# Routing in two halves: six expert slots that run while the other tokens are routed

## The chip, the cores and the metric

The kernel runs on one core of one Trainium2 chip. The metric is device time in microseconds (us). A kernel's figure is the median of its runs. A kernel's profile is one execution; its span is about 1.7 us shorter than the time of that same run.

PE is TensorE's matmul side, PEld its weight loads, DVE is VectorE, ACT ScalarE, POOL GpSimd, SP SyncE, which issues most loads here. PSUM is the memory in which the matmuls leave their results.

## The reference, cut to what matters

```python
# attention: batch 8, heads 8, sequence 576, head width 64; causal, window 64
attn = softmax(mask(scale * q @ k.T)) @ v            # -> x: (8, 576, 512)
# mixture of experts: 8 experts, hidden width 1024
logits = x @ w_gate
local  = sigmoid(x @ w_local)
for b in range(B):
    prev_e = -1
    for s in range(S):
        fresh_e = argmax(logits[b, s])
        e = fresh_e if s == 0 or local[b, s] < 0.5 else prev_e   # goes on along the sequence
        prev_e = e
        p = softmax(logits[b, s])
        out[b, s] = p[e] * (relu(x[b, s] @ w1[e]) @ w2[e])
```

A token's expert can depend on the token before it, so routing is a scan along each sequence. It isn't a scan across batches: the first four batches can be routed before the other four have left attention. That is what makes the change possible.

## The kernel before

There are 4608 tokens: 36 columns of 128. Attention works through nine chunks of 512 tokens, each in four units (pairs of heads). The loop runs `LEAD` units of scores ahead of the values that use them:

```python
def load(sc):                                   # three kinds of buffer, then va
    vtt = vts[sc] = qp.tile([P, HP, SC], F32, name="vtt")             # 2 of these
    kt = kts[sc] = kp.tile([P, HP, SC], F32, name="kt", bufs=4)
    qt = qts[sc] = qp.tile([P, HP, SC], F32, name="qt", bufs=3)
    ...
load(0)
load(1)
...
for i, (sc, hp) in enumerate(units):
    if hp == 0:
        ...
        if sc + 2 < NSC:
            load(sc + 2)
    if i + LEAD < len(units):
        ps[units[i + LEAD]] = scores(*units[i + LEAD])
    ...
    values(sc, hp, ps.pop((sc, hp)), x, g)      # ends with three operations on DVE
    if hp == 0 and sc + 1 < NSC:
        gated = gates(sc + 1)                   # logits of the next chunk, from vtt
    if hp == HP - 1:                            # a chunk is done: its logits, its rows of x
        nc.vector.tensor_reduce(lt[:, 4 * sc:4 * sc + 4, :], ...)
        nc.gpsimd.dma_start(out=xs[...], in_=x...)
```

Then all tokens are routed at once, by some 90 small operations on DVE and a few matmuls. The last step of it is a table: for each place in the experts' list, which token stands there and with what weight. It is a sum of products of one-hot matrices, so it runs on PE, with rows that DVE builds:

```python
for c in range(C):                              # 36 columns of tokens
    rowh = ...                                  # [128, 128]: row of the place, one-hot
    colh = ...                                  # [128, 2, NS]: slot of the place, times token and weight
    nc.tensor.matmul(tab, lhsT=rowh, rhs=colh, start=(c == 0), stop=(c == C - 1))
```

Last come the experts. A slot is 128 tokens of one expert. Blocks of two slots come first, then blocks of one. Each block gathers its rows of x, fetches the expert's two weight matrices (2 MB each; four buffers for either, used in turn), and does two layers:

```python
st = fetch(0)
turn(st)                                        # transposes the gathered rows
for n in range(sure):
    nxt = fetch(n + 1) if n + 1 < sure else None
    hidden(st)                                  # first layer
    if nxt:
        turn(nxt)
    result(st)                                  # second layer, scaled, scattered to out
    st = nxt
rest = [fetch(n) for n in range(sure, NBLK)]    # blocks that may not be needed
with tc.If(used > SURE):
    ...
```

PE's instructions stand in the order of the program (its schedule is set by hand).

## Time and profile before

| what, in the kernel before | us |
|---|---|
| median time of three runs (span of the profiled one, which took 797.36) | 799.2 (795.6) |
| last matmul of attention ends | 139.3 |
| first expert matmul starts | 216.2 |
| last expert matmul ends | 787.4 |
| granted TensorE clock, mean of the span | 0.946 |

Read it as a sum of four terms: attention, a hole, the experts and an end. In the last 571 us PE has no gap, so whatever the change adds to PE's stream there is added to the time; what it takes out of the hole is gained. The lines that show this stand in the prediction.

The transfers that the page lists include the experts' weights (count, size, median us from issue to landing):

```profile
w<-in_w_dram SPq DMA_DIRECT2D x64, 2048.0 KB, 8.4
```

And the very end: the last of these transfers is issued by SP at 773.4 us, 14 us before the last expert matmul ends, and the last result is scattered by POOL at 788.5; the program ends 7 us after that.

```profile
773.43 0.33 SPq L678 DMA_DIRECT2D w<-in_w_dram  x1
```

```profile
788.47 0.98 POOL L714 DMA_INDIRECT out_dram<-y,idx  x1 [13.03 <-ACTq L731]
```

### The profile page before, as it was taken

The numbers are of one execution on the slowest core, as the hardware profiler recorded it, in microseconds if no ns is written. First come the engines' busy times: TensorE is split into PE (matmuls) and PEld (weight loads), VectorE is DVE, ScalarE is ACT, GpSimd is POOL, SyncE is SP. The second block draws the span as 40 slices with busy tenths as digits, with TensorE's granted clock in tenths as the row PEclk, the third lists the DMA queues.
The fourth block names the chain that finished last, engine by engine and source line by source line (L and its number), as shares of the span: only waits on it lengthen the run. The fifth ranks groups of instructions, "written<-read, shape, count | busy, mean of one in ns | idle before, by whom it ended". The sixth has DMA issues, their size and how long they took to land. (4 is left out here: it accounts for less than half of the span.)

```text
span 795.6 us, 12193 instructions
## 1 busy us (share of the span) xinstructions
PE 710.3 (89%) x5295; PEld 509.8 (64%) x5295; DVE 194.3 (24%) x450; ACT 95.3 (12%) x127; POOL 153.3 (19%) x137
## 2 busy tenths in 40 slices
PE   4887888264499999999999999999999999999995
PEld 3666667054277567657756756766877867768673
DVE  5777778794110011001001001000010010100100
ACT  2233333000000000000100000000100001001000
POOL 4565364102201011111121021111111111111000
PEclk9899999555599999999999999999999999999998
DMA  9999993104995544536455364468888888889883
GB/s 334 387 398 395 398 383 121 53 1 176 424 420 221 211 172 161 222 146 221 162 175 222 133 236 174 156 228 330 321 321 312 332 326 312 326 329 325 311 292 120
DMA packets 37570, 204.61 MB, mean 257 GB/s; under 512 B 3485, under 2 KB 3501, under 8 KB 29312
## 3 DMA queue, kind: packets, MB, share of 16 engines
q1 hardware_dynamic: 28320, 173.45, 59.0%
q0 software_dynamic: 9184, 30.24, 9.5%
q8 instruction: 46, 0.75, 0.4%
q14 instruction: 20, 0.16, 0.1%
HBM read 184.80 MB, written 19.92 MB: 257 GB/s over the span
## 5 line engine op out<-in xcount | busy, mean ns | idle before, releaser
L698 PE MATMUL hp<-xt,w 128*128 128x128 f32 (+1 forms) x1856 | 286.3, 315 | 0.0
L698 PEld LDWEIGHTS hp<-xt,w 128*128 128x128 f32 x1856 | 266.0, 192 | 31.3 <-issue 13.4
L710 PE MATMUL yp<-w,h 128*128 128x512 f32 x640 | 279.5, 592 | 0.0
L710 PEld LDWEIGHTS yp<-w,h 128*128 128x128 f32 x640 | 119.5, 190 | 139.3 <-issue 137.0
L702 DVE TENSOR_SCALAR h<-hp 128x512 f32<-128x512 f32 x40 | 27.6, 691 | 521.7 <-issue 401.3
L714 POOL DMA_INDIRECT out_dram<-y,idx x40 | 40.1, 1003 | 305.2 <-ACT y L713 277.8
L672 POOL DMA_INDIRECT xg<-xs,idx x43 | 42.1, 980 | 257.3 <-PE tp L686 202.7
L713 ACT ACTIVATE y<-yp,pw 128x512 f32<-128x512 f32 x40 | 27.5, 687 | 367.6 <-PE yp L710 357.8
L243 PE MATMUL xo<-vb,p 128*64 128x74 f32 x576 | 47.2, 233 | 12.1 <-issue 6.1
L233 DVE TENSOR_TENSOR p<-p,mask 128x1024 f32<-128x1024 f32 x36 | 52.6, 1466 | 15.4 <-ACT p L230 15.4
L214 PE MATMUL sp<-qt,kt 64*64 64x128 f32 (+1 forms) x1296 | 45.6, 278 | 7.8 <-issue 7.8
L704 ACT ACTIVATE h<-hp 128x512 f32<-128x512 f32 x40 | 23.9, 597 | 224.1 <-PE hp L698 224.1
L243 PEld LDWEIGHTS xo<-vb,p 128*64 128x64 f32 x576 | 40.6, 138 | 15.3 <-issue 8.3
L214 PEld LDWEIGHTS sp<-qt,kt 64*64 64x64 f32 x1296 | 39.3, 143 | 17.3 <-issue 15.3
L243 PE MATMUL xo<-va,p 128*64 128x74 f32 x576 | 47.3, 233 | 2.7 <-issue 2.7
L686 PE MATMUL tp<-ident,xg 128*128 128x128 f32 x160 | 25.6, 296 | 21.7 <-DMA xg<-xs,idx 21.7
L230 ACT ACTIVATE p<-sp 128x1024 f32<-128x1024 f32 x36 | 36.9, 1025 | 61.6 <-PE sp L214 50.7
L243 PEld LDWEIGHTS xo<-va,p 128*64 128x64 f32 x576 | 40.6, 138 | 4.1 <-issue 4.1
L686 PEld LDWEIGHTS tp<-ident,xg 128*128 128x128 f32 x160 | 20.3, 153 | 24.7 <-issue 20.8
L201 POOL COPY vb<-va 64x2368 f32<-64x2368 f32 x9 | 27.0, 2999 | 45.9 <-DVE va L198 45.9
L645 PE MATMUL tab<-colh,rowh 128*128 128x86 f32 x72 | 22.4, 467 | 10.7 <-DVE colh L644 10.7
L687 DVE COPY xt<-tp 128x512 f32<-128x512 f32 x40 | 26.5, 681 | 19.1 <-PE tp L686 19.1
(144 smaller groups left out, 210.1 us busy)
## 6 DMA issues: line engine op xcount, KB each, us to landing
w<-in_w_dram SPq DMA_DIRECT2D x64, 2048.0 KB, 8.4
va<-in_v_dram SPq DMA_DIRECT2D x9, 1184.0 KB, 16.9
vtt<-in_vt_dram SPq DMA_DIRECT2D x9, 1024.0 KB, 16.2
xs<-x POOLq DMA_DIRECT2D x9, 1024.0 KB, 9.8
kt<-in_k_dram SPq DMA_DIRECT2D x8, 1024.0 KB, 16.8
qt<-in_q_dram SPq DMA_DIRECT2D x8, 1024.0 KB, 17.0
kt<-in_k_dram SPq DMA_DIRECT2D x4, 256.0 KB, 6.0
qt<-in_q_dram SPq DMA_DIRECT2D x4, 256.0 KB, 5.8
```

Of the source, the lines that this page charges most:

```text
L201: nc.gpsimd.tensor_copy(vb[:WIN], va[:WIN])
L214: nc.tensor.matmul(sp[c * WIN:(c + 1) * WIN, j, a:b], lhsT=kt[h, hp, block * WIN:(block + 1) * WIN], rhs=qt[h, hp, a:b], start=True, stop= ...
L230: nc.scalar.activation(p, sp, Act.Exp, scale=DH ** -0.5)
L233: nc.vector.tensor_tensor(p, p, m.to_broadcast([P, 2, SC]), op=Alu.mult)
L243: nc.tensor.matmul(xo[par * WIN:(par + 1) * WIN, j, s * VW:(s + 1) * VW], lhsT=p[:, j, b * WIN:(b + 1) * WIN], rhs=w[:, s, 2 * hp + j, :], ...
L672: nc.gpsimd.indirect_dma_start(out=x, out_offset=None, in_=xs[:, :], in_offset=bass.IndirectOffsetOnAxis(ap=idx[:, s:s + 1], axis=0))
L686: nc.tensor.transpose(tp[:, kk, :], x[:, kk * P:(kk + 1) * P], ident)
L698: nc.tensor.matmul(hp[:, i, :], lhsT=st["w1"][:, kk, m * P:(m + 1) * P], rhs=st["xt"][:, kk, :n], start=(kk == 0), stop=(kk == DK - 1))
L702: nc.vector.tensor_relu(o, hp)
L710: nc.tensor.matmul(yp, lhsT=st["h"][:, m, i * P:(i + 1) * P], rhs=st["w2"][:, m, :], start=(m == 0), stop=(m == FK - 1))
L713: nc.scalar.activation(y, yp, Act.Copy, scale=pw[:, s:s + 1])
L714: nc.gpsimd.indirect_dma_start(out=out[:, :], out_offset=bass.IndirectOffsetOnAxis(ap=idx[:, s:s + 1], axis=0), in_=y, in_offset=None, bou ...
```

## The change

The intent is to fill the hole. After the fifth of the nine chunks the first four batches are complete. The change makes routing a Python generator with stops (`yield`) in it. The first half's routing advances by one piece after each unit of attention; from the columns it has routed, six full slots are formed (fewer than the batches surely fill). Their rows and weights are fetched while attention still runs, and they are the first six jobs of the experts. The second half is routed between the pieces of those six jobs. For that the experts' weights and attention's q and k share one ring of four buffers, with two spare ones added when attention is over, so six in place of eight; the turned v gets one buffer in place of two, and one buffer of probabilities goes.

The diff, cut to its core:

```diff
+    with ExitStack() as fast:
+        ring = fast.enter_context(tc.tile_pool(name="ring", bufs=4))
+        rt = Router(fast, tc, lt, tabs, ident)
+        ex = Experts(fast, tc, ring, *moe)
+        attention(tc, ring, q, k, v3, vt, xs, lt, ok, wg2s, ident, rt, ex)
+        ex.run(fast, rt)
     bad = const.tile([1, 1], I32, name="bad")
     flag(tc, ok, bad, ident)
-    route(tc, lt, idx, pw, ej, ident)
-    experts(tc, xs, w1, w2, out, idx, pw, ej, ident)
 ...
     def load(sc):
-        vtt = vts[sc] = qp.tile([P, HP, SC], F32, name="vtt")
-        kt = kts[sc] = kp.tile([P, HP, SC], F32, name="kt", bufs=4)
-        qt = qts[sc] = qp.tile([P, HP, SC], F32, name="qt", bufs=3)
+        both = ring.tile([P, 2, HP, SC], F32, name="w")
+        kt, qt = kts[sc], qts[sc] = both[:, 0], both[:, 1]
 ...
+    def turned(sc):
+        vtt = vts[sc] = kp.tile([P, HP, SC], F32, name="vtt", bufs=1)
+        nc.sync.dma_start(out=vtt, in_=vt[:, :, sc * SC:(sc + 1) * SC])
+
+    turned(0)
     load(0)
     load(1)
     gated = gates(0)
+    turned(1)
 ...
         values(sc, hp, ps.pop((sc, hp)), x, g)
         if hp == 0 and sc + 1 < NSC:
             gated = gates(sc + 1)
+            if sc + 2 < NSC:
+                turned(sc + 2)
+        if side:
+            next(side, None)                     # one piece of the first routing
 ...
+            if side is None and 4 * (sc + 1) >= C1:
+                side = rt.first(psum)
+    for _ in side:
+        pass
+    ex.begin()                                   # fetches of the first two jobs
```

The table is built nine columns in one operation. There is one stop between its rows and its matmuls:

```diff
+        for a in range(0, n, 2 * m):             # m = 9; n = 18 in the first, 36 in the second
+            built = []
+            for b in range(a, min(a + 2 * m, n), m):
+                rowh = ...                       # [128, 9, 128] on DVE
+                colh = ...                       # [128, 9, 2, slots] on DVE
+                built.append((rowh, colh))
+            yield
+            for k, (rowh, colh) in enumerate(built):
+                for i in range(m):
+                    nc.tensor.matmul(tab, lhsT=rowh[:, i, :], rhs=colh[:, i, :, :ns], ...)
```

And in the experts a step of the second routing follows each half of a layer:

```diff
+        for i in range(total):
+            ...
+            self.hidden(jobs[i], quiet, step)
+            if i == FIRST - 1:
+                while side:
+                    step()
+                jobs.insert(FIRST, late[0])
+            if i + 1 < total:
+                self.turn(jobs[i + 1], quiet)
+            self.result(jobs[i], step)
+        for n in order[total + 2:]:              # blocks that may not be needed
+            jobs.append(self.fetch(n, spare=n % 3 == 0))
+        with tc.If(used > SURE):
+            ...
```

## The prediction

> **What bounds the kernel now.** I read the page's slices first, then a table of stretches cut where the slices change, then PE's own line of time, then the groups.
>
> The slices (40 of 19.9 us each; tenths busy, then the granted PE clock, then DMA):
>
> ```profile
> PE   4887888264499999999999999999999999999995
> DVE  5777778794110011001001001000010010100100
> PEclk9899999555599999999999999999999999999998
> DMA  9999993104995544536455364468888888889883
> GB/s 334 387 398 395 398 383 121 53 1 176 424 420 221 211 172 161 222 146 221 162 175 222 133 236 174 156 228 330 321 321 312 332 326 312 326 329 325 311 292 120
> ```
>
> Three stages show. Slices 1 to 7 are attention: after the first, PE and DVE are at 7 to 8 tenths, and DMA is full up to the sixth. Slices 8 to 11 are a hole: PE low, the clock at half, DMA empty and then full. From slice 12 to the end PE is at 9 or more, and it sets the time there. The table puts numbers on it (microseconds from the start, busy time of each engine with instruction counts, clock, DMA share, GB/s):
>
> ```profile
> core 0: us, PE busy (x) PEld busy (x) DVE busy (x) ACT busy (x) POOL busy (x), PEclk, DMA share, GB/s
> 92.70:106.80 14.10, 11.48 (x301) 9.42 (x296) 9.23 (x17) 4.98 (x6) 7.64 (x4) 1.00 1.05 397
> 106.80:120.60 13.80, 10.90 (x275) 8.72 (x270) 9.94 (x19) 4.75 (x6) 7.99 (x4) 1.00 0.93 357
> 120.60:139.30 18.70, 16.01 (x433) 13.89 (x433) 15.99 (x31) 5.79 (x7) 7.14 (x4) 1.00 0.32 117
> 140.90:189.50 48.60, 26.37 (x83) 19.86 (x83) 42.09 (x195) 0.44 (x1) 1.95 (x8) 0.52 0.06 22
> 189.50:216.16 26.66, 6.35 (x25) 4.49 (x26) 2.77 (x4) 0.00 (x0) 10.65 (x11) 0.50 0.99 403
> 216.16:527.60 311.44, 311.44 (x1126) 208.35 (x1126) 26.56 (x41) 27.57 (x43) 38.83 (x39) 1.00 0.54 203
> 527.60:787.40 259.80, 259.80 (x1509) 190.60 (x1507) 22.59 (x35) 23.13 (x36) 31.81 (x32) 1.00 0.85 312
> ```
>
> The reader is to see: the last matmul of attention ends at about 139.3. From 140.9 to 189.5 the routing runs, with DVE 42.1 of 48.6 us busy: a chain on DVE. From 189.5 to 216.2 the first weights come in at 403 GB/s and PE only transposes. From 216.2 on PE has no gap at all: 311.4 of 311.4 us and 259.8 of 259.8 us. DMA has room there (0.54 and 0.85). So 216.2 - 139.3 = 76.9 us is a time in which no expert matmul runs, and the rest of the end is PE's sum. PE's timeline shows both sides of the hole, and two blocks of 128 tokens:
>
> ```profile
> 142.36 0.27 PE L110 MATMUL op<-ident,ok 128*1 128x128 f32 x1 [3.02 <-DVE ok L285]
> 148.00 0.59 PE L521 MATMUL tp<-ident,vk 128*36 128x128 f32 x2 [5.37 <-DVE vk L516]
> ...
> 165.75 22.37 PE L645 MATMUL tab<-colh,rowh 128*128 128x86 f32 x72 [10.73 <-DVE colh L644]
> 198.08 1.09 PE L686 MATMUL tp<-ident,xg 128*128 128x128 f32 x4 [9.96 <-DMA xg<-xs,idx]
> ```
>
> ```profile
> 513.86 13.90 PE L710 MATMUL yp<-w,h 128*128 128x512 f32 x32
> 527.59 7.31 PE L698 MATMUL hp<-xt,w 128*128 128x128 f32 x64
> 534.74 0.60 PE L686 MATMUL tp<-ident,xg 128*128 128x128 f32 x4
> 535.17 7.03 PE L710 MATMUL yp<-w,h 128*128 128x512 f32 x16
> 542.04 7.31 PE L698 MATMUL hp<-xt,w 128*128 128x128 f32 x64
> ```
>
> A block of one slot takes 542.04 - 527.59 = 14.45 us of PE. Eleven blocks of two slots take (527.59 - 216.16)/11 = 28.3 us each. Weights are 4 MB a block, so even the small blocks ask for only 312 GB/s.
>
> **What the Trainium skill says.** "TensorE: Matmul & The Clock Gate", Part 1 (The HAM clock gate): after an idle window of about 3.4 us PE runs at half clock, and it needs about as long a busy window to come back. The trace agrees: the clock reads 0.76 in 142 to 144 us, 0.50 from 144, and after the experts start at 216.16 it is still 0.50 to 218 and 1.00 from 219. The same page, "Architectural detail", has ACT and DVE as strict first-in first-out; no view of this trace contradicts it, and I use it twice below: a piece of routing placed on DVE holds back what is queued behind it. "VectorE: DVE Perf Modes", the errata section, gives (N+151)/0.96 ns for a 32-bit tensor_tensor of N columns. The trace agrees for the unhindered mask product of 1024 columns: 1.22 to 1.23 us against 1.22 (the group's mean is 1.47), and for 288 columns 0.457 us against 0.457. I use it for the new 1152-column comparison, which no row shows. "DMA: Bandwidth & Descriptors", "Issuing engines are not separate DMA queues": all queues share 16 engines. So weights asked for early compete with attention's loads; this trace reaches 397 GB/s at a share of 1.05 in attention, full, but only 117 GB/s after 120.6.
>
> **The change part by part.**
>
> Removed from the path: the hole of 76.9 us. Half of the tokens are routed in eight pieces, one after each unit of attention's chunks 5 and 6, so six experts' slots are known before attention ends. Their weights go into the same four 16 KB buffers that q and k leave, of which three are free before the last chunk and the fourth at its end. DMA has room then (0.32 from 120.6). So the wait of 26.7 us for the first weights and rows goes as well.
>
> What comes back before the experts, on DVE in attention. Pieces one to five of the first routing are some 22 operations of 256 columns or fewer, most of 144 or 18; half the columns make 0.31 us (144 columns by the formula) instead of 0.46, and the small ones stay at about 0.16 to 0.2: 2.0 + 1.1 + 0.5 + 1.1 + 0.5 = 5.2 us. The sixth (counts, ranks, places, experts) is some 34 operations, 8.3 us. The seventh builds the one-hot rows: 2 x (1152+151)/0.96 ns = 2.7 us, and six narrow ones of 54 columns at 0.2, together 3.9 us. The last is 0.5 us. Sum 17.9 us. DVE is busy 9.2 and 9.9 us in the two chunks of 14.1 and 13.8 us, so up to 8 us of free time could take some of it, which leaves 9.9 us at least. But routing also takes one of the two PSUM buffers that the values use, so PE must wait for DVE within a unit, and the sixth piece is long enough to stop PE and drop its clock. I take 12 us. The start costs another 2: the turned v of chunk 1 is now asked for after chunk 1's other loads. Total for attention: +14, ending at 153.3.
>
> Changing over: the first expert's transposes (0.6 us), a copy on ACT which stands behind the second routing's exponential, which in turn stands behind attention's last DVE work (1.7 us after the last matmul): +4. Experts start at 157.3 in place of 216.2. So 58.9 us are gained up to here.
>
> What comes back in the experts, on PE. The slots stay at 40 (six, 16 and 18 in place of 22 and 18), but three pairs become six singles: 6 x 14.45 - 3 x 28.3 = +1.8 us. The second routing's matmuls now stand in PE's stream: 72 records for the table at no more than the 7.31/64 = 0.114 us of a hidden matmul = 8.2 us, with transposes and counts about 9. The waits: a job of 14.45 us offers four stops, so one every 3.6 us, and the DVE piece between stop 6 and the table is far longer: 3.3 us for the counts, about 9.4 us for ranks, limits and places over all 36 columns, then a first half of the table, 2 x 1.36 + 6 x (333+151)/0.96 ns = 5.7 us. That is 18.4 us against two stops, 7.3 us: PE waits about 10 us in the second job, and at the half clock after it loses 1 or 2 more. In sum 1.8 + 9 + 11.5 = +22.3 us.
>
> The end: flag's transpose and the last branch now follow the experts. I give it 1 us, as the last scatter (7 to 8 us from 787.4) covers most.
>
> Sum: 76.9 - 14 - 4 - 22.3 - 1 = 35.6 us less. 799.2 - 35.6 = 763.6; I name 762.
>
> **The rivals.**
>
> One: the routing hides fully, in attention and in the experts. For it: DVE is only 10% busy in the experts, the first six jobs leave its share of copies to ACT (23 to 28 us busy of 260 to 311), and PE in attention is at 0.8, so pieces could fall into existing gaps. Against it: the sixth piece has no stop inside. It would make 799 - 76.9 + 4 + 2 + 1.8 + 9 + 1 = 740.
>
> Two: attention turns out bound by DMA, which has fewer buffers for turned v (one for two). The DMA share of 1.05 speaks for it. Against it: no group of PE names a DMA as releaser after the first chunk, and by my count turned v lands some 6 us before it is needed (5.24 MB a chunk at 395 GB/s is 13.3 us, of 13.9). If it loses 3 us a chunk, eight chunks give 24: about 785.
>
> Three: the first jobs wait for weights or rows, since the ring gives a job's buffer back only when the job two before it is done, and the gathers and the SP queue stand in line behind the second routing's tables. Against it: 2 MB land in about 8.4 us (median of the DMA issues), and each has over 13 us from release to use. If it fails, some 5 us a job, up to 20 us: 782.
>
> **Range and chances.** The gain of 76.9 is certain in kind; the terms that give back are 14 (8 to 22), 4 (2 to 7) and 22 (12 to 32). Not all fail together: 748 to 784 holds it 8 times in 10. Faster by over 2% means under 783.2. Chances: 0.90 faster, 0.09 within 2%, 0.01 slower.
>
> **What would show each step.** Right: no stretch of half clock between 140 and 216 beyond a few microseconds; expert matmuls from about 157; weight DMAs issued before 150; DVE busy over 12 us a chunk in chunks 5 and 6, which last about 20 us each; one PE wait of about 10 us on the one-hot tile in the second job; then no gap, blocks at 14.45 and 28.3 us. Wrong: PE waits on turned v or on DMA in attention (rival two), transposes or hidden matmuls waiting on weights or gathered rows in jobs one to six (rival three), or chunks 5 and 6 as short as now (rival one). An expert block longer than 14.45 us with no wait in front would break the premise that PE's sum stays.

## The result, and the profile after

The changed kernel takes 779.83 us, the median of four runs (778.86 to 783.52), against 799.35 us for the kernel before in the same rounds (798.76 to 799.85). The ratio is 0.9765, with a 95% interval from 0.9732 to 0.9797. Here and below a ratio is the mean time of one kernel's fast runs over the mean of the other's in the same rounds, so it is not quite the ratio of the medians. The gain of about 19.5 us is 2.4%; 37 us were expected. The span went from 795.6 to 778.1 us and the mean clock from 0.946 to 0.960.

The slices of the page, 40 of 19.5 us:

```profile
PE   4688884989799999999999999999999999999991
DVE  5476888465500010010010010010010010010010
PEclk9699997799699999999999999999999999999997
DMA  9999995489199966455464463589899888988884
GB/s 331 391 397 395 392 387 208 158 317 347 49 404 424 359 214 237 150 185 206 148 216 177 164 232 144 186 316 340 314 319 345 307 313 338 326 309 320 313 307 182
```

The hole of four slices with the clock at 5 is gone; PE is at 7 or more from the eighth slice to the last but one. But the clock now falls in three places (slices 2, 7 and 8, and 11), DVE is at 8 in slices 5 to 7, and at the very end PE reads 1 in place of 5: something new follows the last matmul.

The same table of stretches as before, now cut where attention's chunks end and where the stages change (microseconds from the start, then the busy time of each engine, clock, DMA share, GB/s):

```profile
core 0: us, PE busy (x) PEld busy (x) DVE busy (x) ACT busy (x) POOL busy (x), PEclk, DMA share, GB/s
96.33:111.03 14.70, 12.79 (x316) 10.19 (x314) 13.84 (x38) 5.98 (x7) 8.58 (x4) 1.00 1.03 378
111.03:134.32 23.29, 11.27 (x234) 9.12 (x229) 20.48 (x64) 3.66 (x4) 6.99 (x5) 0.80 0.65 241
134.32:157.07 22.75, 21.50 (x366) 19.62 (x368) 10.79 (x23) 4.86 (x6) 7.69 (x4) 0.75 0.46 165
165.52:199.53 34.01, 27.35 (x170) 20.48 (x171) 19.84 (x80) 4.47 (x8) 3.85 (x4) 0.96 0.85 334
199.53:207.26 7.73, 7.73 (x37) 7.73 (x37) 2.55 (x4) 0.00 (x0) 0.00 (x0) 0.50 0.00 0
207.26:761.40 554.14, 554.11 (x2721) 391.85 (x2720) 46.52 (x75) 53.60 (x85) 75.45 (x76) 1.00 0.73 270
```

The last row is as before: from 207 us to 761 us PE is busy throughout at the full clock. In the first row, a chunk that takes four pieces of the first routing, all is well too: DVE is busy 13.84 of 14.70 us and the chunk is no longer than before (106.83 - 92.02 = 14.8 us). The second and third rows are two chunks of attention of 23 us each. Chunks took about 14 us before: the reductions that close a chunk, on DVE, give the dates. Before:

```profile
106.83 0.67 DVE L275 TENSOR_REDUCE lt<-g 128x36 f32<-128x288 f32 x1
120.61 0.65 DVE L275 TENSOR_REDUCE lt<-g 128x36 f32<-128x288 f32 x1
133.04 0.67 DVE L275 TENSOR_REDUCE lt<-g 128x36 f32<-128x288 f32 x1
```

After:

```profile
111.03 0.66 DVE L304 TENSOR_REDUCE lt<-g 128x36 f32<-128x288 f32 x1
134.32 0.65 DVE L304 TENSOR_REDUCE lt<-g 128x36 f32<-128x288 f32 x1
157.07 0.68 DVE L304 TENSOR_REDUCE lt<-g 128x36 f32<-128x288 f32 x1
```

From 106.83 to 120.61 is 13.8 us and from 111.03 to 134.32 is 23.3 us, so 9.5 us more; the next chunk went from 12.4 us to 22.75, 10.3 us more. In the first of the two DVE is busy 20.5 of 23.3 us: it is the bound. In the second DVE is busy only 10.8 of 22.75 us while PE is busy 21.5 of them, at a clock of 0.75: there PE is the bound. PE's timeline has the reason. The first line is the start of attention, the second the first table, then the expert stage. The bracket at the end of a line is the time that PE stood idle before it, and what released it:

```profile
27.48 1.93 PE L206 MATMUL xo<-vtt,wg2s 128*32 128x512 f32 x8 [4.12 <-DMA vtt<-in_vt_dram]
```

```profile
134.42 7.82 PE L692 MATMUL xo<-colh,rowh 128*128 128x12 f32 x36 [9.27 <-DVE colh L684]
```

```profile
165.52 3.81 PE L835 MATMUL hp<-xt,w 128*128 128x128 f32 x32 [1.73 <-ACT xt L823]
...
199.53 7.93 PE L692 MATMUL r<-colh,rowh 128*128 128x74 f32 x36 [6.66 <-DVE colh L685]
207.26 5.25 PE L849 MATMUL yp<-w,h 128*128 128x512 f32 x8
212.34 4.14 PE L692 MATMUL r<-colh,rowh 128*128 128x74 f32 x36
216.31 7.36 PE L835 MATMUL hp<-xt,w 128*128 128x128 f32 x64
...
230.81 7.31 PE L835 MATMUL hp<-xt,w 128*128 128x128 f32 x64
...
245.26 7.31 PE L835 MATMUL hp<-xt,w 128*128 128x128 f32 x64
```

The first table's matmuls, 36 records, take 7.82 us: 0.217 us each, at half clock. They stand after a wait of 9.27 us, in which the clock fell (0.50 from 134 to 142 us). The second table has the same: a wait of 6.66 us, 36 records in 7.93 us at half clock, then half a layer at 5.25 us in place of 3.60. Its other half, at full clock, takes 4.14 us. Single-slot jobs take 230.81 - 216.31 = 14.50 us, as before (14.45).

The end (SP's issue of the last transfer, DVE, and POOL's last scatter; a "q" marks the engine's own queue):

```profile
761.40 0.33 SPq L809 DMA_DIRECT2D w<-in_w_dram  x1
762.42 0.98 POOL L855 DMA_INDIRECT out_dram<-y,idx  x1 [13.03 <-ACTq L902]
770.91 0.28 DVE L128 TENSOR_REDUCE lo<-op 1x1 f32<-1x128 f32 x1 [15.63 <-DMA w<-in_w_dram]
```

The last expert matmul ends at 761.4, the last scatter is issued at 762.4, but the reduction for `flag` starts only at 770.9, after 15.6 us of idle DVE, released by a DMA that fills a weight buffer. The program ends 16.7 us after the last expert matmul, against 8.2 us before. The page counts six more weight transfers than before, 70 for 64: three pairs became six singles, so there are three more jobs with two transfers each. That is traffic, and no wait for it is seen.

```profile
w<-in_w_dram SPq DMA_DIRECT2D x70, 2048.0 KB, 8.8
```

Put side by side with the terms of the prediction (all in us, of the spans):

| term | before | after | difference | predicted |
|---|---|---|---|---|
| attention, to its last matmul | 139.3 | 163.8 | +24.5 | +14 |
| from there to the first expert matmul | 76.9 | 1.7 | -75.2 | -72.9 |
| experts, to their last matmul | 571.2 | 595.9 | +24.7 | +22.3 |
| end | 8.2 | 16.7 | +8.5 | +1 |
| span | 795.6 | 778.1 | -17.5 | -35.6 |

The gain is 18.1 us short. Attention is 10.5 us of that, the end 7.5, the experts 2.4, and the change-over gives 2.3 back.

### The profile page after: what moved, and what is told of

Same layout as the page of the kernel before. It is cut to its first block, busy times and chain, and to the rows that moved or that the text cites. A ratio compares the mean times of both kernels' runs of the same rounds, so it can differ in the third digit from the quotient of the medians.

```text
span 778.1 us, 12674 instructions
## 1 busy us (share of the span) xinstructions
PE 710.0 (91%) x5533; PEld 519.4 (67%) x5533; DVE 185.1 (24%) x415; ACT 103.1 (13%) x142; POOL 155.4 (20%) x137
## 4 chain that ended last, share of the span: by engine, by line
PE 87%; DVE 5%; DMA 4%; issue 2%; ACT 1%; POOL 0%; POOLq 0%; DVEq 0%; ACTq 0%
PE hp L835 36%; PE yp L849 35%; PE xo L262 5%; PE sp L233 5%; PE tp L822 2%; DMA vtt<-in_vt_dram 2%; PE r L692 2%; PE xo L206 1%; DMA w<-in_w_dram 1%; PE xo L692 1%; DVE p L252 1%; PE xo L216 1%; DMA wg2s<-in_wg_dram 1%; DVE rowh L676 1%; DVE x L271 1%
## 5 line engine op out<-in xcount | busy, mean ns | idle before, releaser
L835 PEld LDWEIGHTS hp<-xt,w 128*128 128x128 f32 x2048 | 272.5, 191 | 28.6 <-issue 13.9
L839 DVE TENSOR_SCALAR h<-hp 128x512 f32<-128x512 f32 x34 | 23.5, 691 | 495.8 <-issue 362.0
L803 POOL DMA_INDIRECT xg<-xs,idx x43 | 42.2, 981 | 225.5 <-PE tp L822 193.2
L262 PEld LDWEIGHTS xo<-vb,p 128*64 128x64 f32 x576 | 42.2, 142 | 14.2 <-issue 5.8
L233 PE MATMUL sp<-w 64*64 64x128 f32 (+1 forms) x1296 | 46.6, 285 | 4.2 <-issue 4.2
L233 PEld LDWEIGHTS sp<-w 64*64 64x64 f32 x1296 | 40.6, 147 | 14.2 <-issue 11.5
L841 ACT ACTIVATE h<-hp 128x512 f32<-128x512 f32 x46 | 27.5, 597 | 165.3 <-PE hp L835 153.3
L206 PE MATMUL xo<-vtt,wg2s 128*32 128x512 f32 x72 | 12.7, 747 | 14.2 <-DMA wg2s<-in_wg_dram 8.3
L271 DVE TENSOR_TENSOR x<-xo,allr 128x512 f32<-128x512 f32 x36 | 24.4, 678 | 0.0
L822 PE MATMUL tp<-ident,xg 128*128 128x128 f32 x160 | 22.8, 273 | 0.0
L221 POOL COPY vb<-va 64x1776 f32<-64x1776 f32 x9 | 22.0, 2444 | 0.5
## 6 DMA issues: line engine op xcount, KB each, us to landing
w<-in_k_dram SPq DMA_DIRECT2D x8, 1024.0 KB, 10.5
```

Of the source, the lines that this page charges most:

```text
L233: nc.tensor.matmul(sp[c * WIN:(c + 1) * WIN, j, a:b], lhsT=kt[h, hp, block * WIN:(block + 1) * WIN], rhs=qt[h, hp, a:b], start=True, stop= ...
L262: nc.tensor.matmul(xo[par * WIN:(par + 1) * WIN, j, s * VW:(s + 1) * VW], lhsT=p[:, j, b * WIN:(b + 1) * WIN], rhs=w[:, s, 2 * hp + j, :], ...
L271: nc.vector.tensor_tensor(x[:, :, hp].rearrange("p c j d -> p j c d"), o[:, :, :, :DH], rr.to_broadcast([P, 2, 4, DH]), op=Alu.mult)
L803: nc.gpsimd.indirect_dma_start(out=x, out_offset=None, in_=self.xs[:rows, :], in_offset=bass.IndirectOffsetOnAxis(ap=idx[:, s:s + 1], axis=0))
L822: nc.tensor.transpose(tp[:, kk, :], x[:, kk * P:(kk + 1) * P], self.ident)
L835: nc.tensor.matmul(hp[:, i, :], lhsT=st["w1"][:, kk, m * P:(m + 1) * P], rhs=st["xt"][:, kk, :n], start=(kk == 0), stop=(kk == DK - 1))
```

## The experiments

The theory after reading the trace (A): four separate terms, each on the path that sets the end. The end waits for a transfer that nobody needs; the start waits for the turned v of chunk 1; the second table's wait, and the half clock that the wait causes, cost about 12 us in the experts; and the first table's matmuls stand fully in PE's stream in attention. The rival (B) for each: the waits shown are not on the path, and something behind them (the scatter at the end, the transfers at the start, DVE's work as a whole) would take their place. Each experiment up to the warm clock changes one thing in the changed kernel; the finer pieces and the last two kernels change several. The mark is the changed kernel's time, 779.83 us; all results were correct. The kernel before took 798.99 us in the rounds of the first group (the tile, the fetch, the start, the first table's stops), 799.59 us in those of the second (the second table's stops, the warm clock, the doubled table, the finer pieces) and 799.10 us in those of the last two kernels.

### The flag's tile in memory of its own

The tile `lo`, one element that `flag` writes, lies in memory that the experts' buffers have given back. So its first use may wait until the last transfer into them has landed. The edit puts it in the pool that lives through the whole kernel.

```diff
+    lo = const.tile([1, 1], F32, name="lo")
-    flag(tc, ok, bad, ident)
+    flag(tc, ok, lo, bad, ident)
 def flag(...):
-    fp = ctx.enter_context(tc.tile_pool(name="fl", bufs=1))
-    lo = fp.tile([1, 1], F32, name="lo")
```

> The changed kernel, with flag's one-element tile taken from the constants' pool instead of a pool opened after the experts. In the changed kernel the last expert matmul ends at 761.4 us, flag's reduction runs at 770.9, and the profile puts its wait down to a weight DMA issued at 761.4. Theory A (flag's tile lies in memory that the weight ring has left, so it must wait until the last, unused weights have landed): the reduction runs within 2 us of flag's transpose at about 762.1, and the end comes earlier, but only by 3 to 6 us (about 775), because the program still has to wait for that DMA to land at about 770.8. Theory B (the later place of flag, its chain PE to DVE to register to branch, costs the time by itself): the reduction still runs late or the end does not move: 779 to 781.

Measured: 776.21 us (775.56 to 778.21), ratio 0.9720 [0.9701, 0.9738]; 3.6 us less than the changed kernel. The reduction now waits for PE's transpose alone, and starts 7.5 us earlier:

```profile
763.38 0.28 DVE L127 TENSOR_REDUCE lo<-op 1x1 f32<-1x128 f32 x1 [8.32 <-PE op L126]
```

The reason is right, but only 3.6 of the 8.5 us came back. The unneeded transfer itself is still under way when everything else is done: from 765 to 768 us none of PE, DVE, ACT and POOL is busy, and the DMA engines move 399 GB/s.

### The unneeded weights fetched in the branch that needs them

```diff
-        for n in order[total + 2:]:
-            jobs.append(self.fetch(n, spare=n % 3 == 0))
         with tc.If(used > SURE):
+            for n in order[total + 2:]:
+                jobs.append(self.fetch(n, spare=n % 3 == 0))
             for st in jobs[total:]:
```

> The changed kernel, with the one fetch that waits for the last expert's weights to be done (the last of the three optional blocks) moved into the branch that uses it, which is not taken here; flag and its tile are left as they are. Theory A (unused weights, issued at 761.4 behind the last matmul and landing 9.4 us later, hold up flag and the end): the last weight DMA is issued before 750, flag's reduction runs at about 763, the tail after the last matmul falls from 16.7 to about 8.5 us, the time to about 771.5 (minus 8). Theory B (the place of flag): the tail stays near 16, the time near 780.

Measured: 770.24 us (769.19 to 772.79), ratio 0.9642 [0.9620, 0.9665]; 9.6 us less. The last weights are asked for at 746.3 and not at 761.4, and the reduction needs no tile of its own to be early:

```profile
760.89 0.28 DVE L128 TENSOR_REDUCE lo<-op 1x1 f32<-1x128 f32 x1 [6.69 <-PE op L126]
```

So the whole end term is this one transfer, which the order of the buffers had put behind the last expert matmul: the one that it fills comes free only when the last job's second layer is through. The kernel before fetched its optional blocks too, but with two more buffers its last transfer left 14 us before the last expert matmul ended, as shown; that the two buffers are the reason follows from the program, and no run tests it. (The edit gains 9.6 us where the end had lost 8.5; the two profiled runs also differ by about 1 us ahead of it, which is the size of a run's own scatter.)

### The turned v of chunk 1 ahead of that chunk's other loads

```diff
     turned(0)
     load(0)
-    load(1)
     ...
     gated = gates(0)
     turned(1)
+    load(1)
```

> The changed kernel, with the second chunk's turned v asked for before the second chunk's q, k and v instead of after them; one buffer for turned v stays. In the changed kernel PE waits 4.1 us for it at 23.4 to 27.5 us, and the clock is at half from 20 to about 34. Theory A (the order of the first loads costs the 4.2 us by which chunk 0 ends later, 40.8 against 36.6): the wait goes, chunk 0 ends at 36.5 to 37.5, and the time falls by 3 to 4.5, to about 776. Theory B (one buffer for turned v instead of two slows attention in general): the gain of the start is lost again by chunk 4, whose end stays at 96 us, and the time stays at 779 to 780.

Measured: 775.52 us (773.63 to 778.72), ratio 0.9710 [0.9688, 0.9731]; 4.3 us less, with the widest scatter of the single edits: the five runs cover 5.1 us, and the profiled one is the fastest of them. In the trace the matmuls that waited 4.12 us start 4.2 us earlier and wait for nothing:

```profile
23.32 1.94 PE L205 MATMUL xo<-vtt,wg2s 128*32 128x512 f32 x8
```

The first chunk ends at 36.7 us, as in the kernel before (36.6), and not at 40.8. The 4.2 us are kept to the end: attention's last chunk closes at 159.9 in place of 165.3. Later gates do wait for a turned v here, four times and 6.0 us in all up to 96 us, but the chunks are no longer for it: chunk 4, counted from 0, ends at 92.24, as in the kernel before (92.02).

### Two more stops ahead of the first table's matmuls

The 9.27 us wait suggests that the rows are not ready when PE comes for them. Two empty stops let PE do two more units of attention first.

```diff
-            yield
+            for _ in range(1 + (hold[0] if a == 0 else hold[1])):
+                yield
...
-        yield from self.table(psum, slice(0, C1), FIRST, lo, hi, vec, tabs["idx1"], tabs["pw1"])
+        yield from self.table(psum, slice(0, C1), FIRST, lo, hi, vec, tabs["idx1"], tabs["pw1"], (2, 0))
```

> The changed kernel, with the first routing's table matmuls two units of attention later (two more empty stops between building the one-hot rows on DVE and the matmuls); no work is added or taken away. In the changed kernel PE waits 9.3 us for the last of these rows and then does 36 matmuls at half clock in 7.8 us. Theory A (PE's in-order queue meets the table matmuls before DVE has built the rows): the wait falls below 2 us, the 36 matmuls take about 4.2 us at full clock, and attention's last matmul comes 9 to 13 us earlier than at 163.6; the time falls to about 768. Theory B (DVE's added work of 18 us is what lengthens chunks 6 and 7, wherever PE waits): the wait moves to other places (mask product, PSUM buffers), attention's end moves by less than 4 us, the time stays above 775. Between them, DVE becomes the bound of those units: 770 to 775.

Measured: 779.11 us (778.22 to 779.49), ratio 0.9745 [0.9729, 0.9762]; the same as the changed kernel. Here the theory fell. The wait on the rows is gone from the list of PE's waits (96 to 165 us; in total, times, longest), and others stand in its place:

```profile
PE xo L262 <- DVE x L271: 5.7, 3, 3.3
...
PE xo L595 <- DVE x L271: 1.8, 1, 1.8
```

L271 is the last DVE operation of a unit's values, which frees the PSUM buffer that PE needs next. PE can't run ahead of DVE by more than those two buffers, so it waits for DVE's queue in any case, for rows or for a buffer. The table of stretches says why (same columns as above):

```profile
124.00:128.00 4.00, 2.30 (x68) 2.11 (x68) 3.93 (x18) 1.38 (x2) 0.68 (x1) 1.00 0.00 0
128.00:132.00 4.00, 1.82 (x40) 1.32 (x40) 4.00 (x16) 0.00 (x0) 0.36 (x1) 1.00 0.78 258
132.00:136.00 4.00, 3.16 (x48) 2.21 (x40) 4.00 (x10) 1.61 (x2) 0.39 (x1) 0.60 1.00 379
```

DVE is busy 3.93 to 4.00 of 4.00 us in each, and PE 1.82 to 3.16. In this chunk DVE's sum is the bound, and a wait moved is, for the most part, a wait kept: from the end of the first chunk to that of the last, attention takes 122.5 us in place of 124.6. The table's 36 records still took 7.86 us at half clock, later.

### The first table's matmuls issued twice

Is the first table's time on PE on the path at all? The matmuls run twice, the second run overwriting the first with the same result.

```diff
+            for r in range(2 if ns == FIRST else 1):
                 for k, (rowh, colh) in enumerate(built):
                     for i in range(m):
                         nc.tensor.matmul(tab, lhsT=rowh[:, i, :], rhs=colh[:, i, :, :ns], ...)
```

> The changed kernel, with the first routing's 36 table matmul records issued twice (the second set starts the sum anew, so the result is the same). It doubles one suspected cost. Theory A (the first table's matmuls are wholly on the path, at half clock, as everything in attention stands behind them): the second set takes another 7.8 us, as matmuls of 12 columns did not bring the clock back in 7.8 us, and attention's end and the time move by 7 to 8.5, to about 788. Theory B (they fill time in which DVE would be the bound anyway): under 3 us. If the clock comes back in the second set: 4 to 5 us.

Measured: 787.02 us (786.06 to 788.17), ratio 0.9837 [0.9821, 0.9854]; 7.2 us more. PE's timeline has the doubled group at 15.50 us, so 7.7 us more:

```profile
133.05 15.50 PE L693 MATMUL xo<-colh,rowh 128*128 128x12 f32 x72 [9.27 <-DVE colh L684]
```

Nearly every microsecond that the table takes longer on PE is a microsecond of the end; how much would come back if the table were gone, no run shows. Not one of the 72 records ran at the full clock, although PE was busy without a gap for 15.5 us.

### More stops ahead of the second table's matmuls

The same edit as for the first table, with three more stops ahead of the first half's matmuls and one more ahead of the second's: `(0, 0)` for the first table and `(3, 1)` for the second. Here PE has expert work to do in the meantime, and it isn't tied to DVE by a buffer, for ACT takes the copies of these jobs.

> The changed kernel, with the second routing's table matmuls later in the experts: three more empty stops before the first 18 columns' matmuls and one more before the last 18. In the changed kernel PE waits 6.7 us for the one-hot rows in the second job and then does 36 table matmuls at half clock in 7.9 us and half an expert's second layer in 5.3 in place of 3.4. DVE is nearly empty there, so, unlike in the test of the first routing, nothing should take the wait's place. Theory A (PE's order against DVE's single long piece): no wait above 1 us, both groups of table matmuls at full clock, about 4.1 us each, 12 us gained, time about 768. Theory B (the experts' first jobs wait for something else as well, weights or rows): a new wait appears, gain under 5 us, time above 775.

Measured: 768.03 us (766.88 to 770.11), ratio 0.9599 [0.9583, 0.9615]; 11.8 us less. No wait, and both halves at the full clock:

```profile
199.38 7.31 PE L836 MATMUL hp<-xt,w 128*128 128x128 f32 x64
206.52 4.14 PE L693 MATMUL r<-colh,rowh 128*128 128x74 f32 x36
...
217.80 4.13 PE L693 MATMUL r<-colh,rowh 128*128 128x74 f32 x36
```

### The clock kept up through the wait

How much of that is the wait, and how much the half clock after it? Here the wait stays, but PE is kept busy in it with 27 matmuls whose result is thrown away.

```diff
+                bank = psum()
+                if ns == NS:
+                    for _ in range(27):
+                        nc.tensor.matmul(bank[:, :P], lhsT=self.tri, rhs=self.ones, start=True, stop=True)
-                tab = psum()[:, :2 * ns]...
+                tab = bank[:, :2 * ns]...
```

> The changed kernel, with 27 idle-filling fp32 matmuls (54 records, about 6.2 us at full clock, into the table's own bank, overwritten afterwards) put in front of the second routing's first table matmul, so that PE works in the time in which it waits 6.7 us. The wait itself stays filled, only the clock should change. Theory A (half of the cost of that stop is the clock that drops in the wait): the 36 table matmuls behind it take about 4.2 in place of 7.9 us, the next half layer 3.5 in place of 5.3, time about 774.5 (minus 5.5). Theory B (the table's matmuls are slow there for another reason, the operands or the bank): no change, or 6 us slower.

Measured: 773.90 us (773.50 to 774.48), ratio 0.9675 [0.9659, 0.9692]; 5.9 us less. The filler lies where the wait was, and the table behind it runs at full clock:

```profile
192.62 6.19 PE L692 MATMUL r<-ones,tri 128*128 128x128 f32 x54
199.37 4.24 PE L696 MATMUL r<-colh,rowh 128*128 128x74 f32 x36 [0.55 <-DVE colh L685]
203.44 3.64 PE L853 MATMUL yp<-w,h 128*128 128x512 f32 x8
```

7.93 us became 4.24 and 5.25 us became 3.64: together 5.3 us, near the 5.9 measured. So of the 11.8 us of this stop about half is the wait itself and half the cold clock.

### The first routing in finer pieces

If DVE's long sixth piece and the table cause the stalls in attention, finer cuts should help: fifteen pieces over fifteen units in place of eight, rows two stops ahead of their matmuls, the table in two halves that DVE adds.

```diff
+        yield                                    # within the gate, after the scan, after the experts, after the limits
...
-        yield from self.table(psum, slice(0, C1), FIRST, ...)
+        for b in range(0, C1, PIECE):
+            rowh, colh = self.rows(slice(0, C1), b, PIECE, FIRST, lo, hi)
+            yield
+            yield
+            tab = psum()[:, :2 * FIRST]...
+            for i in range(PIECE):
+                self.nc.tensor.matmul(tab, lhsT=rowh[:, i, :], rhs=colh[:, i, :, :FIRST], ...)
+            if b:
+                vec.tensor_tensor(acc, acc, tab, op=Alu.add)
+            else:
+                vec.tensor_copy(acc, tab)
```

> The changed kernel, with the first routing cut into 15 pieces over 15 of the 16 units that are left, in place of 8 over 8; each nine columns' rows are built two stops before their matmuls, and the two sums of nine are added on DVE. The later-matmuls test showed DVE busy 4.0 of 4.0 us from 96 to 136 us. Theory A (DVE is full in chunks 5 and 6, and has some 2 us a chunk left in chunk 7 and little in 8; the table costs extra as it stands in one block at half clock): chunk 6 falls from 23 to about 18 us, chunk 7 from 23 to about 17, attention ends 8 to 11 us earlier, time about 770. Theory B (what is added to DVE lengthens attention wherever it stands, and the table too): chunks 7 and 8 take up what chunk 6 gives, gain under 3 us, time 777 or more.

Measured: 782.70 us (781.43 to 783.02), ratio 0.9789 [0.9772, 0.9805]. The median is 2.9 us above the changed kernel's, but the runs of the two overlap (778.86 to 783.52 there), so it isn't shown to be slower; it is no gain. B had the time (777 or more), but not the reason. Attention itself did gain, nearly as A had it: chunks 6 and 7 fell to 17.8 and 16.5 us, and the last chunk closes at 158.7 in place of 165.3. But the six slots' table was now ready only at 156.9, so the rows were gathered late, and PE waited for them at the change-over and then ran at half clock (6.47 us for half a layer in place of 3.81):

```profile
163.64 1.09 PE L858 MATMUL tp<-ident,xg 128*128 128x128 f32 x4 [6.03 <-DMA xg<-xs,idx]
165.45 6.47 PE L871 MATMUL hp<-xt,w 128*128 128x128 f32 x32 [0.72 <-ACT xt L859]
```

The first expert matmul starts at 165.45, where it started at 165.52. The gain of 6.7 us was spent on the new wait of 6.03.

### The edits together

The fetch in its branch, the flag's tile, the start and the second table's stops in one kernel.

> Four of the edits that each won alone, in one kernel: the last unused weights fetched only in the branch not taken (-9.6 alone), the flag's one-element tile in memory that is never given back (-3.6 alone), the turned v of chunk 1 asked for before chunk 1's other loads (-4.3), and three more empty stops before the second table's first half and one before its second (-11.8). If the costs are separate terms of a sum, as my accounting has them, they add, but the first two are one wait and count once: 779.8 - 9.6 - 4.3 - 11.8 = 754, range 751 to 758, and no wait of over 1 us on PE between 165 us and the end. The flag's tile may add up to 0.5. If the start's gain is only passed on to DVE's full stretch in chunks 5 and 6 or to the weights' arrival (rival), about 4 less of gain: 758 to 760. I expect 754.

Measured: 756.89 us (755.10 to 757.49), ratio 0.9464 [0.9452, 0.9477]; 22.9 us less than the changed kernel and 42.2 us less than the kernel before. The sum of the single gains was 25.7. Of the expected waits none is left: in this kernel's list of PE's waits from 165 us to the end one line remains:

```profile
PE op L126 <- PEq L900: 0.3, 1, 0.3
```

The time is within the range expected, 751 to 758.

What is missing lies in attention, but not where the rival looked for it. The first hidden matmul starts at 163.45, only 2.1 us earlier than in the changed kernel; in the profile of the start's edit alone it started at 160.06. Chunks 5 and 6 together take the same in these two profiles (37.5 and 37.3 us). The combined kernel loses 2.6 us in chunk 1 (15.8 us in place of 13.2), where the gates wait 3.2 us for a turned v in place of 2.3 and then run at half clock, and 2.2 us in chunks 7 and 8, which stay unexplained. But the profile of the start's edit is that of its fastest run, and this one is the second slowest of five, so part of the difference is scatter. I do not take the 4.3 us of the single edit as a constant.

### The same with a finer first routing

With the four edits, and the finer routing in twelve pieces, so that its table is ready some units earlier.

> As the kernel with the four edits, and the first routing in twelve pieces in place of eight (its long sixth piece cut in four, its table in two halves with one stop between), so that it ends about three units earlier than the fifteen pieces of the earlier run, some 10 us before attention's end, and the first rows are gathered in time. If the late gather alone took the gain of the finer pieces (theory A): attention ends 4 to 7 us earlier than in the kernel with four edits, the first hidden matmul starts that much earlier, and the time is 748 to 751. If DVE, full through chunks 5 and 6, sets attention's end whatever the cuts (rival B), within 1.5 us of the kernel with four edits, or slower by 1 to 2 for the added operations. I expect 750.

Measured: 756.05 us (754.77 to 762.11), ratio 0.9490 [0.9459, 0.9520]. Four of six runs lie between 754.8 and 756.5, two at 762, and the interval overlaps that of the kernel with four edits. In the profile the rows come in time (a wait of 0.5 us), and the first expert matmul starts at 161.3, 2.1 us earlier. But its table still waits 4.0 us on its rows and still runs at half clock. I had expected 4 to 7 us earlier, and the rival, that DVE's sum sets attention's end, at most 1.5: this lies between the two. In time the two kernels can't be told apart. Why two runs took 6 us more stays open: their clock, 0.973, hardly differs from the others' 0.974 to 0.980.

The kernel with four edits is therefore the version that I would keep: 5.4% under the kernel before by its ratio.

## Why the prediction was right or wrong

The direction was right and the range, 748 to 784, holds 779.83, 4 us from its upper edge; the point of 762 was 18 us too low. That the times of the second and third rivals, 785 and 782, lie nearer is luck, for what they describe did not happen.

**Bound and hole: right.** The 76.9 us without expert matmuls became 1.7. The change-over was sized at 4 and is 1.7: the copy on ACT (at 164.39) ran before the second routing's exponential (167.04), and not behind it as forecast.

**Attention, +14 predicted, +24.5 measured: the mechanism was right for DVE, and a term of PE was left out.** The prediction took 17.9 us of DVE work, of which at least 9.9 would not fit, and named 12. The measured 9.5 us in the chunk where DVE is full agree with the lower figure, in part by luck: DVE's busy time in chunks 5 and 6 rose by 15.2 us (13.84 + 20.48 against 9.23 + 9.94), but 3.7 us of these chunks it still stood idle. The run with two more stops shows that it is DVE's sum and not the place of the wait. Of the signs, chunks 5 and 6 were to last about 20 us each; chunk 5 stayed at 14.7, and chunks 6 and 7 took 23.3 and 22.8. What the sum lacked is the first table's 18 matmuls: the prediction gave the second table a term on PE and the first one none. They are 7.8 us at half clock in a chunk that grew by 10.3, and the doubled table shows that they lie fully on the path (7.2 us for 7.7 more). This omission is the largest single error. The start was sized at 2 and is 4.2; the edit to it gained 4.3.

One thing was overlooked in DVE's sum. Four operations of the first routing (lines 568, 579, 614 and 709 of the changed kernel) took 1.23, 0.68, 1.59 and 0.67 us, 4.2 us together. The first three took 0.41, 0.18 and 0.31 us in the second routing, with the same shapes. Each of the four ran beside one of POOL's copies of the values and ended within 0.3 us after it, so some 3 us of DVE's time here may be POOL's doing; no run tests it.

**The experts, +22.3 predicted, +24.7 measured: right in kind, and right in size by two errors that cancel.** The wait was sized at 10 us and is 6.7. The table was sized at 9 us, at full clock, and "1 or 2 more" for the half clock after the wait; its first half took 7.9 us in place of 4.1, and the layer after it 1.7 us more. The small matmuls of the second routing come to nearly 2 us in place of 0.8. The warm-clock run shows that the cold clock is 5 to 6 us of this term, three to four times what I gave it. The trace before held a warning: there the clock did come back for the experts' matmuls, as the prediction says, but the table ran for 22.4 us without a gap at 0.50. The premise that blocks keep their 14.45 us held (14.50).

**The end, +1 predicted, +8.5 measured: wrong.** I let the last scatter cover it. I had not asked where in the ring the fetch of the optional block stands: with six buffers in place of eight it gets its own only when the last job's second layer is done, so a 2 MB transfer that no one reads (8.8 us at the median) starts with the end itself. Two runs, one of which takes away only the flag's wait and one the transfer, show it.

**The rivals.** The first, that routing hides fully, is out: chunks 6 and 7, counted from 0, are 23 us long. The second, attention bound by DMA from the smaller buffers, appears only at the start (4 us) and nowhere later in the changed kernel's list of waits. Its count of 5.24 MB a chunk was a little low: the transfers that the page lists, 1184 KB and four times 1024 KB, are 5.41 MB, 13.7 us at 395 GB/s, so there was less room than the prediction said. The third, weights or rows that come late in jobs one to six, did not occur in the changed kernel; the finer routing then made just that wait, 6 us at the change-over.

## What to carry to other kernels

When work is moved under other work, give it a term on every engine that it uses, and on each with the clock that the wait ahead of it leaves: here a table of 4 us of matmuls cost 8 us behind a wait, twice. Follow the buffers of a shared ring to the very last transfer, for a prefetch that is not needed became the end of the program here. And before a wait is moved, look whether the engine named in it is full: in attention, where DVE was, another wait took its place; in the experts, where PE had independent work, a few more stops took the whole cost away.

## What the Trainium skill lacked or had wrong

- "TensorE: Matmul & The Clock Gate", Part 1, gives about 3.4 us of sustained activity until the clock returns. For the experts' matmuls these runs come near it (the clock is back 2 to 3 us after 216.2 us in the kernel before, where transposes ran ahead of them). For the tables they do not: 7.8 us and even 15.5 us of gapless table matmuls left the clock at half (0.50 in the changed kernel's stretches from 134 to 138, 138 to 142 and 142 to 144 us, and in the doubled one's from 133 to 148.5), and the clock came back only when other matmuls followed. The table of the kernel before is alike: 22.4 us without a gap at 0.50. These tables load a new 128-column matrix for each 12, 74 or 86 columns that they stream. Whether that ratio is the cause no run here tells; the filler of 128 columns each in the wait did hold the clock that was up.
- The same page, "LDWEIGHTS (loading the stationary operand)", has the load's time follow its columns over 1.2, so 107 ns for 128, and no figure for the half clock. The tables measure 0.115 us from record to record at full clock (4.14 us for 36) and 0.217 to 0.220 us at half, nearly the same for 12 as for 74 streamed columns.
- No page that I found says that a tile laid in memory that another pool has given back can wait for that pool's last transfer: here the flag's reduction waited until 770.9 us for weights nobody read, which made 3.6 us of the time, and with the transfer itself 9.6.
